# Another order for the early work of a gated-linear-attention and GLU kernel, with some casts and products on other engines

## Chip, cores and metric

One core of one Trainium2 chip. The metric is the device time of a run in microseconds (us); of several runs the median is taken.

## The reference

An attention with a decaying state, and a gated linear unit behind it. B, H, S, D are 4, 8, 768, 48; the 3072 tokens have 384 channels, and the hidden width is 1536.

```python
for t in range(S):
    state = alpha[:, :, t, :, None] * state + np.einsum('bhd,bhe->bhde', k[:, :, t], v[:, :, t])
    y[:, :, t] = np.einsum('bhd,bhde->bhe', q[:, :, t], state)
x = y.transpose(0, 2, 1, 3).reshape(B * S, H * D)
gate = 1 / (1 + np.exp(-(x @ w_gate)))
out = (gate * (x @ w_val)) @ w_out
```

Everything is float32, and the weights reach the kernel as float64 words.

## The kernel before

**Units.** The attention runs in 24 units: six groups g of 512 tokens by four pairs p of heads. A unit u = 4 g + p loads decay, K and Q (L464, on SyncE's queue), and V (L468, or L472 for the first four). `decays` makes the decay products: a scan from the right (G, L406), a maximum and a reciprocal at chunk borders (L408, L409), a scan from the left (F, L410), the chunk decay (`dec`, L412), and K times G (L414). Q times F follows (L480). On TensorE come the transposition of K (L427), the scores (L492), and the state additions (L497). VectorE masks the scores (L505) and carries the state from chunk to chunk (L520), GpSimd multiplies the states by `dec` (L558 in the first four units, L531 in the next four, L658 later), and TensorE makes the outputs (L571 and L576, or L542 and L546). The first eight units ("early") use chunks of 128 tokens, the rest (`late`) chunks of 64.

**Steps.** The gated unit runs in 72 steps, 12 for a group of tokens. A step multiplies 128 of the 1536 hidden columns: 18 matmuls for gate and value (L693, by way of L236), the sigmoid (L698, ScalarE), the product (L700, VectorE), its split into two float32r halves (L701 ScalarE, L702 VectorE), and nine matmuls back to 384 channels (L710). Every product is made of three matmuls of such halves.

**Weights.** Twelve weight tiles are made in the first 120 us, tile 0 in three pieces of 384 columns and the others in two of 576 (`weight_piece`). A piece is a load (L360), a cast of the upper bits (L363 on VectorE if the piece stands in `CASTS`, else L365 on ScalarE), a shift-and-or (L368, VectorE), a cast (L371, ScalarE) and a subtraction (L378, VectorE).

**Order.** Every piece of work is added to a `Plan` with its engine, its cost in us, a due time or none, and what it reads and writes. `Plan.order` then replays the engines with these costs: each engine takes the ready part with the earliest latest start, and the order of the replay is the order in which each engine's queue is written. Parts with `port` set take turns in the replay: one that would begin while another has the port waits for it. `SHIFTS` adds so many us to the latest start of single parts, which are numbered in the order in which they were added. `QUERIES` and `KEYS` name the early units whose L480 and L414 run on VectorE; elsewhere they run on GpSimd. 29 matmuls on constants (L681) stand in the plan: eight at its start, the others wherever TensorE has nothing ready. Nothing is reordered on the chip: every engine goes through its queue in order.

The lines of the change: costs at L363, L365, L408, L409, L412, L416, L514, L531, L558, L578, L611 and L649; the tuples at L804 to L807.

Of the kernel before, what the change touches and what calls it, by code (L numbers as in the profile page):

```python
# [37 lines left out]
CH, EH = T // C, T // E  # L38
# [163 lines left out]
def pool_(n):  # L202
    return 0.08 + n / 445
# [36 lines left out]
def chunked(ctx, tc, rows, vc, vh, vg, weights_in, out, const, ident, flags, weights, within):  # L240
    nc = tc.nc
    sb = ctx.enter_context(tc.tile_pool(name="sb", bufs=1))
    ps = ctx.enter_context(tc.tile_pool(name="ps", bufs=1, space=bass.MemoryType.PSUM))
    plan = Plan()
# [46 lines left out]
    for tag in ("w11", "w8"):  # L291
        nm, t = borrow(tag, WF + 2)
# [53 lines left out]
    def weight_piece(f, key):  # L346
        cuts = (0, DM, 2 * DM, WF) if f == 0 else (0, WF // 2, WF)
        over = before(f"w{f}") if f >= 6 else []
        for i, (lo, hi) in enumerate(zip(cuts, cuts[1:])):
            n = hi - lo  # L350
            rn, raw = (r_raw if f < 7 else r_raw3).next() if f < NF - 1 else raws[i]
            raw = raw[:, 0:2 * n + 2]
            lower = raw[:, 1:1 + 2 * n].rearrange("p (m j) -> p m j", j=2)[:, :, 0]
            most = raw[:, 2:2 * n + 2].bitcast(BF16).rearrange("p (m h) -> p m h", h=4)[:, :, 0]
            tn, top = (r_top if f < 8 else r_top1).next()
            top = top[:, 0:n]
            high = top.bitcast(F16).rearrange("p (m h) -> p m h", h=2)[:, :, 1]
            ru, rl, rt = (rn, "u"), (rn, "l"), (tn, "a")
            kk = key
            plan.add("sync", (0.475, P * n * 8 / RATE), None, lambda raw=raw, lo=lo, n=n: nc.sync.dma_start(  # L360
                out=raw.bitcast(U16), in_=ahead(weights_in, f, lo, n)), writes=[ru, rl])
            if (f, i) in CASTS:
                plan.add("vector", 0.01 + n / 960, kk, lambda high=high, most=most: nc.vector.tensor_copy(out=high, in_=most), [ru], [rt], port=True)  # L363
            else:
                plan.add("scalar", 0.08 + n / 500, kk, lambda high=high, most=most: nc.scalar.copy(out=high, in_=most), [ru], [rt])  # L365
            high, low = (weights_part(f, part, lo, hi) for part in range(2))
            word = raw[:, 0:n]
            plan.add("vector", 0.07 + n / 960, kk, lambda lower=lower, top=top, word=word: nc.vector.scalar_tensor_tensor(  # L368
                out=word, in0=lower, scalar=13, in1=top, op0=ALU.logical_shift_right, op1=ALU.bitwise_or), [rt, ru], [rl], port=True)
# [29 lines left out]
    def decays(u, size, t, inn, tin):  # L399

        n, nch = T, T // size
        a0, az, kT = tin[:, 0:nch], tin[:, A_Z:A_K], tin[:, A_K:A_Q]
        over = ["later"] if size == E else []
        (gn, G), (fn, F), (g0n, G0), (decn, dec) = r_G.next(), r_F.next(), r_G0.next(), r_dec.next()
        G0, dec = G0[:, 0:nch], dec[:, 0:nch]
        plan.add("vector", scan(n), t["G"], lambda: nc.vector.tensor_tensor_scan(  # L406
            out=G[:, ::-1], data0=az[:, n:0:-1], data1=d1g[size], initial=0.0, op0=ALU.mult, op1=ALU.add), [(inn, "a"), *over], [gn], port=True)
        plan.add("vector", 0.1, t["G"], lambda: nc.vector.tensor_tensor(out=G0, in0=G[:, 0:n:size], in1=tiny[:, 0:nch], op=ALU.max), [gn], [g0n], port=True)  # L408
        plan.add("vector", 0.1, t["G"], lambda: nc.vector.reciprocal(out=d1f[:, 0:n:size], in_=G0), [g0n], ["d1f"])  # L409
        plan.add("vector", scan(n), after(t["G"], 0.01), lambda: nc.vector.tensor_tensor_scan(  # L410
            out=F, data0=az[:, 0:n], data1=d1f, initial=0.0, op0=ALU.mult, op1=ALU.add), ["d1f", (inn, "a")], [fn], port=True)
        plan.add("vector", 0.1, t["dec"], lambda: nc.vector.tensor_tensor(out=dec, in0=a0, in1=G[:, 0:n:size], op=ALU.mult), [gn, (inn, "a")], [decn], port=True)  # L412
        e = "vector" if u in KEYS else "gpsimd"
        plan.add(e, vec(n) if u in KEYS else pool_(n), t["kt"], lambda: getattr(nc, e).tensor_tensor(  # L414
            out=kT, in0=kT, in1=G, op=ALU.mult), [gn, (inn, "r")], [(inn, "k")], port=True)
        plan.add("scalar", 0.2, t["flag"], lambda: nc.scalar.copy(out=starts[:, u, 0:nch], in_=G[:, 0:n:size]), [gn], [("start", u)])  # L416
        return fn, F, decn, dec

    def bound(u, t, fn, F):
# [39 lines left out]
    def unit(u, g, p, t):  # L459

        n, nch = T, CH
        inn, tin = r_in.next()
        for lo, hi, marks in ((0, A_K, "a"), (A_K, WIDTH, "rkq")) if u < NP else ((0, WIDTH, "arkq"),):
            plan.add("sync", (0.475, P * (hi - lo) * 4 / RATE), t["load"], lambda lo=lo, hi=hi: nc.sync.dma_start(  # L464
                out=tin[:, lo:hi], in_=rows[g, p, :, lo:hi]), writes=[(inn, m) for m in marks])
        if g:
            vn, v = r_v.next()
            plan.add("sync", (0.475, P * CH * 2 * D * 4 / RATE), after(t["load"], 0.2), lambda: nc.sync.dma_start(  # L468
                out=v.rearrange("p c j e -> p (c j e)"), in_=vc[g, p]), writes=[(vn, "v")])
        else:  # L470
# [60 lines left out]
        plan.add("gpsimd", pool_(nch * D), t["sd"], lambda: nc.gpsimd.tensor_tensor(  # L531
            out=sd, in0=st[:, 0:nch], in1=dec.rearrange("p (c o) -> p c o", o=1).broadcast_to([P, nch, D]), op=ALU.mult), [sn, decn], [(sdn, x) for x in range(4)])

        yield
# [17 lines left out]
    def in_place(p, t, qT, inn, vw, A, sd, st, dec):  # L552
# [2 lines left out]
        sd = sd.rearrange("p j c e -> p (j c e)")[:, 0:CH * 2 * D].rearrange("p (c e) -> p c e", e=2 * D)  # L555
        for j in range(2):
            r = slice(R * j, R * j + R)
            plan.add("gpsimd", pool_(CH * D), t["sd"], lambda j=j, r=r: nc.gpsimd.tensor_tensor(  # L558
                out=sd[r, :, D * j:D * j + D], in0=st[r, 0:CH], in1=dec[r].rearrange("p (c o) -> p c o", o=1).broadcast_to([R, CH, D]), op=ALU.mult),
                [sn, decn], [(sdn, 2 * j), (sdn, 2 * j + 1)])  # L560
        blocks = [divmod(3 * p + i, 4) for i in range(3)]
# [16 lines left out]
        plan.add("tensor", (0.9, 0.5), t["out"], from_states, [(inn, "q"), *((sdn, x) for x in range(4))], banks)  # L578
# [10 lines left out]
    def late(u, g, p, t):  # L589
# [18 lines left out]
            plan.add("sync", (0.475, R * EH * D * 4 / RATE), after(t["more"], 0.2), lambda j=j: nc.sync.dma_start(  # L608
                out=vs[other[j], j].rearrange("p c e -> p (c e)"), in_=vh[g, p, j]), writes=[(vsn, j)])
        for j in range(2):  # L610
            plan.add("vector", 0.71, t["q"], lambda j=j: nc.vector.tensor_tensor(  # L611
                out=A[own[j], j], in0=A[own[j], j], in1=F[own[j]], op=ALU.mult), [fn], [(an, 2 + j)], port=True)
        bound(u, t, fn, F)

# [31 lines left out]

        st, sn = sts[p], ("st", p)
        done = EH if u >= EARLY + NP else CH
        plan.add("gpsimd", 0.28, t["S"], lambda: nc.gpsimd.tensor_copy(out=st[:, 0, :], in_=st[:, done, :]), writes=[sn])  # L649

        def states():
            for c in range(EH):
# [148 lines left out]


SUMS = ()
CASTS = ((0, 2), (3, 1), (5, 0), (5, 1), (7, 0), (7, 1), (10, 1))  # L804
QUERIES = (0, 4, 5, 6)
KEYS = (0,)
SHIFTS = ((0, -5), (37, -1), (40, -2), (45, -1), (49, -1), (62, 1), (96, 2), (118, 1), (124, -1), (126, 2), (127, 2), (134, -1), (142, -2), (152, 4), (153, -6), (164, 13), (192, -2), (222, -5), (227, 1), (235, -1), (261, -4), (280, 2), (289, -5), (303, 4), (304, 3), (307, 7), (314, 17), (323, 3), (328, 4), (331, 13), (340, -6), (350, 4), (378, 12), (389, 2), (414, 8), (421, 7), (422, 9), (435, 5), (436, -1), (443, 9), (448, 4), (500, 3), (543, 1), (552, 4), (643, -1), (784, -4), (817, 4), (849, 2), (885, 2))  # L807
WARM = 29
APART = 24

# [143 lines left out]
```

## Time and profile before

| | |
|---|---|
| median of 3 runs | 552.58 us (552.45 to 552.87) |
| the profiled execution | 552.85 us, of which the span is 551.0 us |
| TensorE busy | 538.3 us, 98% of the span |
| VectorE busy | 328.7 us, 60% |
| ScalarE busy | 179.2 us, 33% |
| GpSimd busy | 93.8 us, 17% |
| HBM traffic | 41.16 MB read, 4.72 MB written |
| mean granted clock of TensorE | 0.993 |

The profile is one execution. PE is TensorE's matmuls, PEld its weight loads, DVE is VectorE, ACT ScalarE, POOL GpSimd, SP SyncE (it issues the loads). Times count from the start of the span. PEclk is the granted clock of TensorE as a share of its full one. A row of the timeline gives start, duration, engine, line, operation, out<-in by tile names, and how many instructions it merges; in square brackets stands the engine's idle time before it and whose end it waited for. A tile can bear the name of the memory that it borrows (`first_w`, `first_x`).

### The profile page before, as it was taken

The page shows a single profiled execution, that of the slowest core. Times are in us where ns is not written, and L with a number is a line of the kernel's source. Part 1 is how long each engine was busy: PE and PEld are TensorE (multiplying, and loading weights), DVE is VectorE, ACT ScalarE, POOL GpSimd, SP SyncE. Part 2 cuts the span into 40 slices and gives each one's busy share as a digit, 9 for nine tenths or more (in the row PEclk, how much of TensorE's full clock was granted, in tenths as well). Part 3 has the DMA queues.
Part 4 walks back from the last instruction along what each step waited for, and adds up shares of the span by engine and source line. Part 5 has one row for each costly group of instructions (what it writes and reads, how often), then busy time and mean ns, then how long its engine had stood idle before and what let it go on. Part 6 is the DMA issues. An engine that isn't in the chain of part 4 may idle for free.

```text
span 551.0 us, 10327 instructions
## 1 busy us (share of the span) xinstructions
PE 538.3 (98%) x4215; PEld 435.3 (79%) x4215; DVE 328.7 (60%) x629; ACT 179.2 (33%) x337; POOL 93.8 (17%) x113
## 2 busy tenths in 40 slices
PE   8998999999999999999999999999999999999994
PEld 4776877888888888888888888888888888888883
DVE  7789998977657567648547557566566342222221
ACT  2445645552223232323223323223323222211221
POOL 5650132002202202112012022022021010000000
PEclk9998999999999999999999999999999999999998
DMA  8645875721402311403203303213211000100001
GB/s 312 259 130 171 262 253 150 229 89 61 151 20 83 101 43 59 159 1 102 90 13 101 136 23 103 66 36 101 104 56 49 2 16 16 57 0 1 0 2 62
DMA packets 21576, 50.57 MB, mean 92 GB/s; under 512 B 3344, under 2 KB 8464, under 8 KB 21520
## 3 DMA queue, kind: packets, MB, share of 16 engines
q1 hardware_dynamic: 21520, 49.83, 28.0%
q8 instruction: 35, 0.57, 0.4%
q14 instruction: 21, 0.17, 0.1%
HBM read 41.16 MB, written 4.72 MB: 83 GB/s over the span
## 4 chain that ended last, share of the span: by engine, by line
PE 96%; DVE 1%; POOL 1%; issue 0%; ACT 0%; POOLq 0%; ACTq 0%
PE gv L236 54%; PE po L710 28%; PE gv L670 3%; PE gv L427 2%; PE at L624 2%; PE gv L681 1%; PE at L630 1%; PE po L576 1%; PE at L492 1%; PE gv L542 1%; PE gv L546 1%; PE po L571 1%; PE gv L497 0%; POOL first_w L480 0%; PE po L681 0%
## 5 line engine op out<-in xcount | busy, mean ns | idle before, releaser
L236 PE MATMUL gv<-x,w 128*128 128x512 f32 x1296 | 316.1, 390 | 0.0
L236 PEld LDWEIGHTS gv<-x,w 128*128 128x128 f32 x1296 | 242.5, 188 | 52.2 <-issue 0.8
L700 DVE TENSOR_TENSOR gv<-gv,sg 128x512 f32<-128x512 f32 x72 | 50.3, 699 | 156.7 <-PE gv L236 153.0
L710 PE MATMUL po<-hh,w 128*128 128x512 f32 x432 | 115.8, 399 | 1.0 <-ACT w L371 0.9
L710 PEld LDWEIGHTS po<-hh,w 128*128 128x128 f32 x432 | 80.1, 189 | 18.8 <-ACT w L371 1.0
L701 ACT CAST hh<-gv 128x512 fp32r<-128x512 f32 x72 | 42.2, 586 | 152.5 <-DVE gv L700 145.5
L658 POOL TENSOR_TENSOR vs<-st,dec 64x384 f32<-64x384 f32 x32 | 36.4, 1139 | 277.1 <-DVE st L653 261.5
L698 ACT ACTIVATE sg<-gv 128x512 f32<-128x512 f32 x72 | 43.0, 597 | 120.2 <-PE gv L236 119.6
L702 DVE TENSOR_TENSOR hl<-gv,hh 128x512 fp32r<-128x512 f32 x72 | 49.6, 689 | 24.5 <-ACT hh L701 22.4
L710 PE MATMUL po<-hl,w 128*128 128x512 f32 x216 | 63.7, 393 | 0.0
L710 PEld LDWEIGHTS po<-hl,w 128*128 128x128 f32 x216 | 40.7, 189 | 8.6
L653 DVE SCALAR_TENSOR_TENSOR st<-st,dec,at 128x48 f32<-128x48 f32 x128 | 33.9, 265 | 4.2
L414 POOL TENSOR_TENSOR in<-in,G 128x512 f32<-128x512 f32 x21 | 28.7, 1367 | 39.3 <-DVE G L406 33.0
L406 DVE TENSOR_TENSOR_SCAN G<-in,d1g 128x512 f32<-128x512 f32 x22 | 34.1, 1551 | 2.1 <-DMA in<-in_rows_dram 2.1
L640 DVE TENSOR_TENSOR A<-at,mask 64x256 f32<-64x256 f32 x64 | 26.9, 420 | 7.8 <-PE at L630 7.4
L410 DVE TENSOR_TENSOR_SCAN F<-in,d1f 128x512 f32<-128x512 f32 x22 | 27.8, 1264 | 0.6
L611 DVE TENSOR_TENSOR A<-A,F 64x512 f32<-64x512 f32 x32 | 23.4, 731 | 0.5
L420 ACT ACTIVATE F<-F 128x512 f32<-128x512 f32 x23 | 14.5, 631 | 16.9 <-DVE A L611 15.3
L670 PE MATMUL gv<-A,vs 128*48 128x64 f32 (+1 forms) x512 | 17.6, 221 | 0.0
L670 PEld LDWEIGHTS gv<-A,vs 128*48 128x48 f32 (+1 forms) x512 | 15.2, 123 | 2.8 <-DVE A L640 2.2
L431 ACT COPY kn<-gv 128x512 f32<-128x512 f32 x21 | 12.3, 586 | 12.2 <-PE gv L427 10.0
L438 ACT COPY yt<-gv 128x512 f32<-128x512 f32 x20 | 11.7, 586 | 11.7 <-PE gv L670 7.4
(130 smaller groups left out, 338.7 us busy)
## 6 DMA issues: line engine op xcount, KB each, us to landing
in<-in_rows_dram SPq DMA_DIRECT2D x16, 516.5 KB, 3.8
raw<-in_w_dram SPq DMA_DIRECT2D x14, 577.0 KB, 4.6
first_w<-in_w_dram SPq DMA_DIRECT2D x8, 577.0 KB, 4.5
out_dram<-raw SPq DMA_DIRECT2D x18, 256.0 KB, 2.3
A<-in_rows_dram SPq DMA_DIRECT2D x32, 128.0 KB, 3.3
v<-in_vc_dram SPq DMA_DIRECT2D x20, 192.0 KB, 4.3
in<-in_rows_dram SPq DMA_DIRECT2D x4, 772.5 KB, 5.8
vs<-in_vh_dram SPq DMA_DIRECT2D x32, 96.0 KB, 2.8
```

The lines of the kernel that those rows point to most:

```text
L236: nc.tensor.matmul(out=dst, lhsT=lhs(a, i), rhs=rhs(b, i), start=(n == 0 and i == 0), stop=(n == len(todo) - 1 and i == NK - 1))
L406: plan.add("vector", scan(n), t["G"], lambda: nc.vector.tensor_tensor_scan(out=G[:, ::-1], data0=az[:, n:0:-1], data1=d1g[size], initial=0 ...
L410: plan.add("vector", scan(n), after(t["G"], 0.01), lambda: nc.vector.tensor_tensor_scan(out=F, data0=az[:, 0:n], data1=d1f, initial=0.0, o ...
L414: plan.add(e, vec(n) if u in KEYS else pool_(n), t["kt"], lambda: getattr(nc, e).tensor_tensor(out=kT, in0=kT, in1=G, op=ALU.mult), [gn, ( ...
L653: nc.vector.scalar_tensor_tensor(out=st[:, c + 1, :], in0=st[:, c, :], scalar=dec[:, c:c + 1], in1=pas[c % 2][1][:, T // 2 + c // 2 * D:T ...
L658: plan.add("gpsimd", pool_(EH * D), t["sd"], lambda j=j: nc.gpsimd.tensor_tensor(out=vs[own[j], j], in0=st[own[j], 0:EH], in1=dec[own[j]]. ...
L670: nc.tensor.matmul(out=py[R * j:R * j + D, cs], lhsT=vs[r, j, c, :], rhs=A[r, j, cs], start=True, stop=True)
L698: plan.add("scalar", act(T), first(0.3), lambda: nc.scalar.activation(out=sg, in_=got["g"][1][:, 0:T], func=AF.Sigmoid), [got["g"][0]], [sgn])
L700: plan.add("vector", vec(T), first(0.4), lambda: nc.vector.tensor_tensor(out=pv, in0=pv, in1=sg, op=ALU.mult), [sgn], [pvn])
L701: plan.add("scalar", act(T), first(0.45), lambda: nc.scalar.copy(out=hh, in_=pv), [pvn], [hhn])
L702: plan.add("vector", vec(T), first(0.5), lambda: nc.vector.tensor_tensor(out=hl, in0=pv, in1=hh, op=ALU.subtract), [pvn, hhn], [hln])
L710: nc.tensor.matmul(out=pso_now[m][1][:, 0:T], lhsT=weights.part("o", b, f)[:, m * P:(m + 1) * P], rhs=h[a][:, 0:T], start=(f == 0 and i == ...
```

## The change

It alters costs by which the plan orders, the `port` mark of VectorE's weight casts, the engine of some casts and products, and all of `SHIFTS` but two entries. No operation, tile or transfer is added or taken away. The diff, with the shifts cut after the first entries (before there are 49, after 58):

```diff
             if (f, i) in CASTS:
-                plan.add("vector", 0.01 + n / 960, kk, lambda ...: nc.vector.tensor_copy(out=high, in_=most), [ru], [rt], port=True)
+                plan.add("vector", 0.04 + n / 1700, kk, lambda ...: nc.vector.tensor_copy(out=high, in_=most), [ru], [rt])
             else:
-                plan.add("scalar", 0.08 + n / 500, kk, lambda ...: nc.scalar.copy(out=high, in_=most), [ru], [rt])
+                plan.add("scalar", n / 800, kk, lambda ...: nc.scalar.copy(out=high, in_=most), [ru], [rt])
...
-        plan.add("vector", 0.1, t["G"], ... op=ALU.max ...)
-        plan.add("vector", 0.1, t["G"], ... reciprocal ...)
+        plan.add("vector", 0.08, t["G"], ... op=ALU.max ...)
+        plan.add("vector", 0.09, t["G"], ... reciprocal ...)
...
-        plan.add("vector", 0.1, t["dec"], ...)
+        plan.add("vector", 0.07, t["dec"], ...)
...
-        plan.add("scalar", 0.2, t["flag"], ... starts ...)
+        plan.add("scalar", 0.14, t["flag"], ... starts ...)
...
-            plan.add("gpsimd", 0.28, t["G"], ... st[:, nch, :] ...)
+            plan.add("gpsimd", 0.18, t["G"], ... st[:, nch, :] ...)
...
-        plan.add("gpsimd", pool_(nch * D), t["sd"], ...)
+        plan.add("gpsimd", 0.57, t["sd"], ...)
...
-            plan.add("gpsimd", pool_(CH * D), t["sd"], ...)
+            plan.add("gpsimd", 0.57, t["sd"], ...)
...
-        plan.add("tensor", (0.9, 0.5), t["out"], from_states, ...)
+        plan.add("tensor", (1.0, 0.5), t["out"], from_states, ...)
...
-            plan.add("vector", 0.71, t["q"], ... in1=F[own[j]] ...)
+            plan.add("vector", 0.61, t["q"], ... in1=F[own[j]] ...)
...
-        plan.add("gpsimd", 0.28, t["S"], ... st[:, done, :] ...)
+        plan.add("gpsimd", 0.18, t["S"], ... st[:, done, :] ...)
...
-CASTS = ((0, 2), (3, 1), (5, 0), (5, 1), (7, 0), (7, 1), (10, 1))
-QUERIES = (0, 4, 5, 6)
-KEYS = (0,)
-SHIFTS = ((0, -5), (37, -1), (40, -2), (45, -1), (49, -1), (62, 1), (96, 2), (118, 1), (124, -1), (126, 2), ...
+CASTS = ((0, 0), (0, 1), (3, 0), (4, 0), (5, 1), (6, 0), (6, 1), (7, 0), (8, 0))
+QUERIES = (0, 1, 2, 6)
+KEYS = (0, 2, 4, 6)
+SHIFTS = ((13, -1), (43, 3), (63, -2), (64, 1), (65, -4), (69, 1), (84, -1), (97, -2), (98, -2), (99, -1), (107, -1), (125, 13), (128, 2), ...
```

In numbers of parts, 0 to 152 belong to the fill matmuls' first entries and units 0 to 3, 153 to 277 to the weight pieces, and those from 278 on to the later units and the steps. Of the 58 shifts 13, 14 and 31 lie in these three.

## Rows read from the trace of the kernel before

**Rows 1.** The page: TensorE's busy time, and the chain that ended last, by engine.

```profile
PE 538.3 (98%) x4215; PEld 435.3 (79%) x4215; DVE 328.7 (60%) x629; ACT 179.2 (33%) x337; POOL 93.8 (17%) x113
...
PE 96%; DVE 1%; POOL 1%; issue 0%; ACT 0%; POOLq 0%; ACTq 0%
```

**Rows 2.** Windows: length, PE, PEld, DVE, ACT, POOL busy, PEclk, DMA share, GB/s.

```profile
20.00:25.00 5.00, 4.08 (x69) 3.39 (x64) 4.24 (x10) 1.41 (x4) 4.04 (x4) 1.00 0.59 209
...
45.00:50.00 5.00, 3.40 (x36) 2.49 (x37) 5.00 (x12) 2.99 (x7) 0.00 (x0) 0.85 0.47 126
50.00:55.00 5.00, 5.00 (x21) 3.80 (x21) 4.92 (x11) 2.78 (x4) 1.00 (x2) 0.81 0.69 227
...
7.00:20.00 13.00, 13.00 (x183) 9.12 (x183) 9.72 (x22) 4.69 (x11) 7.03 (x8) 1.00 1.03 397
5.00:55.00 50.00, 46.01 (x505) 33.88 (x505) 44.08 (x92) 21.99 (x45) 20.16 (x26) 0.97 0.63 220
...
57.00:130.00 73.00, 72.99 (x511) 58.41 (x512) 62.58 (x110) 38.43 (x69) 11.98 (x11) 1.00 0.59 191
130.00:544.00 414.00, 413.90 (x3165) 340.23 (x3163) 217.95 (x419) 115.13 (x219) 57.51 (x57) 1.00 0.18 57
```

**Rows 3.** Timeline, unit 1: its Q product, fill matmuls, scores and first mask.

```profile
14.08 2.17 POOL L480 TENSOR_TENSOR in<-in,F 128x512 f32<-128x512 f32 x1 [2.35 <-DVE dec L412]
...
16.10 1.04 PE L681 MATMUL gv<-ident 128*128 128x512 bf16 x4
...
17.06 0.37 PE L492 MATMUL gv<-in 48*128 48x128 f32 x1
...
18.26 0.69 DVE L505 TENSOR_TENSOR A<-gv,mask 128x512 f32<-128x512 f32 x1 [1.94 <-PE at L492]
```

**Rows 4.** Timeline, unit 2: its Q product, scores and masks.

```profile
20.88 2.10 POOL L480 TENSOR_TENSOR first_w<-first_w,first_x 128x512 f32<-128x512 f32 x1 [2.36 <-DVE dec L412]
...
23.04 1.16 PE L492 MATMUL gv<-first_w 48*128 48x128 f32 x16 [0.85 <-POOL first_w L480]
...
24.23 1.29 DVE L505 TENSOR_TENSOR first_x<-gv,mask 128x512 f32<-128x512 f32 x2 [0.65 <-PE gv L492]
```

**Rows 5.** Timeline: a K product of unit 4 and `dec` beside it; `dec` alone (unit 0).

```profile
33.31 1.69 POOL L414 TENSOR_TENSOR in<-in,G 128x512 f32<-128x512 f32 x1 [1.95 <-DVE G L406]
33.80 1.23 DVE L412 TENSOR_TENSOR dec<-in,G 128x4 f32<-128x4 f32 x1
...
4.96 0.16 DVE L412 TENSOR_TENSOR dec<-in,G 128x4 f32<-128x4 f32 x1
```

**Rows 6.** One line's instructions (ns min/median/max): L414 on either engine, L480 on VectorE.

```profile
L414 POOL TENSOR_TENSOR in<-in,G x21: 1267/1290/1693, 8.7 to 403.9; 128x512 f32<-128x512 f32 x21
L414 DVE TENSOR_TENSOR in<-in,G x1: 661/661/661, 5.2 to 5.2; 128x512 f32<-128x512 f32 x1
...
L480 DVE TENSOR_TENSOR in<-in,F x4: 667/686/687, 8.4 to 70.6; 128x512 f32<-128x512 f32 x4
```

**Rows 7.** Casts on either engine, GpSimd's state products (one line each); then a timeline.

```profile
L363 DVE CAST first_w<-first_w x2: 382/441/500, 46.2 to 55.9; 128x384 f16<-128x384 bf16 x1, 128x576 f16<-128x576 bf16 x1
...
L365 ACT CAST top<-raw x7: 633/854/877, 14.1 to 117.2; 128x576 f16<-128x576 bf16 x6, 128x384 f16<-128x384 bf16 x1
...
L531 POOL TENSOR_TENSOR vs<-st,dec x4: 506/591/882, 39.4 to 92.8; 128x192 f32<-128x192 f32 x4
...
50.39 0.50 DVE L363 CAST first_w<-raw 128x576 f16<-128x576 bf16 x1
50.62 0.59 POOL L531 TENSOR_TENSOR vs<-st,dec 128x192 f32<-128x192 f32 x1 [10.40 <-DVE st L520]
```

**Rows 8.** Timeline: unit 4's scores, the first back products, and six such at the end.

```profile
45.07 1.16 PE L492 MATMUL at<-in 48*128 48x128 f32 x16 [0.77 <-DVE in L480]
...
48.21 3.20 PE L710 MATMUL po<-hh,w 128*128 128x512 f32 x6 [0.86 <-ACT w L371]
...
537.62 1.52 PE L710 MATMUL po<-hh,w 128*128 128x512 f32 x6
```

More of the change, by code (lines that the diff above doesn't have):

```diff
@@ L362, in weight_piece @@
             if (f, i) in CASTS:
-                plan.add("vector", 0.01 + n / 960, kk, lambda high=high, most=most: nc.vector.tensor_copy(out=high, in_=most), [ru], [rt], port=True)
+                plan.add("vector", 0.04 + n / 1700, kk, lambda high=high, most=most: nc.vector.tensor_copy(out=high, in_=most), [ru], [rt])
             else:
-                plan.add("scalar", 0.08 + n / 500, kk, lambda high=high, most=most: nc.scalar.copy(out=high, in_=most), [ru], [rt])
+                plan.add("scalar", n / 800, kk, lambda high=high, most=most: nc.scalar.copy(out=high, in_=most), [ru], [rt])
             high, low = (weights_part(f, part, lo, hi) for part in range(2))
@@ L407, in decays @@
             out=G[:, ::-1], data0=az[:, n:0:-1], data1=d1g[size], initial=0.0, op0=ALU.mult, op1=ALU.add), [(inn, "a"), *over], [gn], port=True)
-        plan.add("vector", 0.1, t["G"], lambda: nc.vector.tensor_tensor(out=G0, in0=G[:, 0:n:size], in1=tiny[:, 0:nch], op=ALU.max), [gn], [g0n], port=True)
-        plan.add("vector", 0.1, t["G"], lambda: nc.vector.reciprocal(out=d1f[:, 0:n:size], in_=G0), [g0n], ["d1f"])
+        plan.add("vector", 0.08, t["G"], lambda: nc.vector.tensor_tensor(out=G0, in0=G[:, 0:n:size], in1=tiny[:, 0:nch], op=ALU.max), [gn], [g0n], port=True)
+        plan.add("vector", 0.09, t["G"], lambda: nc.vector.reciprocal(out=d1f[:, 0:n:size], in_=G0), [g0n], ["d1f"])
         plan.add("vector", scan(n), after(t["G"], 0.01), lambda: nc.vector.tensor_tensor_scan(
             out=F, data0=az[:, 0:n], data1=d1f, initial=0.0, op0=ALU.mult, op1=ALU.add), ["d1f", (inn, "a")], [fn], port=True)
-        plan.add("vector", 0.1, t["dec"], lambda: nc.vector.tensor_tensor(out=dec, in0=a0, in1=G[:, 0:n:size], op=ALU.mult), [gn, (inn, "a")], [decn], port=True)
+        plan.add("vector", 0.07, t["dec"], lambda: nc.vector.tensor_tensor(out=dec, in0=a0, in1=G[:, 0:n:size], op=ALU.mult), [gn, (inn, "a")], [decn], port=True)
         e = "vector" if u in KEYS else "gpsimd"
@@ L415, in decays @@
             out=kT, in0=kT, in1=G, op=ALU.mult), [gn, (inn, "r")], [(inn, "k")], port=True)
-        plan.add("scalar", 0.2, t["flag"], lambda: nc.scalar.copy(out=starts[:, u, 0:nch], in_=G[:, 0:n:size]), [gn], [("start", u)])
+        plan.add("scalar", 0.14, t["flag"], lambda: nc.scalar.copy(out=starts[:, u, 0:nch], in_=G[:, 0:n:size]), [gn], [("start", u)])
         return fn, F, decn, dec
@@ L513, in unit @@
         if g:
-            plan.add("gpsimd", 0.28, t["G"], lambda: nc.gpsimd.tensor_copy(out=st[:, 0, :], in_=st[:, nch, :]), writes=[sn])
+            plan.add("gpsimd", 0.18, t["G"], lambda: nc.gpsimd.tensor_copy(out=st[:, 0, :], in_=st[:, nch, :]), writes=[sn])
         else:
@@ L530, in unit @@
         sd = sd[:, 0, 0:CH, :]
-        plan.add("gpsimd", pool_(nch * D), t["sd"], lambda: nc.gpsimd.tensor_tensor(
+        plan.add("gpsimd", 0.57, t["sd"], lambda: nc.gpsimd.tensor_tensor(
             out=sd, in0=st[:, 0:nch], in1=dec.rearrange("p (c o) -> p c o", o=1).broadcast_to([P, nch, D]), op=ALU.mult), [sn, decn], [(sdn, x) for x in range(4)])
@@ L557, in in_place @@
             r = slice(R * j, R * j + R)
-            plan.add("gpsimd", pool_(CH * D), t["sd"], lambda j=j, r=r: nc.gpsimd.tensor_tensor(
+            plan.add("gpsimd", 0.57, t["sd"], lambda j=j, r=r: nc.gpsimd.tensor_tensor(
                 out=sd[r, :, D * j:D * j + D], in0=st[r, 0:CH], in1=dec[r].rearrange("p (c o) -> p c o", o=1).broadcast_to([R, CH, D]), op=ALU.mult),
@@ L576, in from_scores @@
                     nc.tensor.matmul(out=at(i, c), lhsT=vw[:, c, lo:lo + 32], rhs=A[:, j, c * C:(c + 1) * C], start=False, stop=(c == CH - 1 and (i, j) != (1, 0)))
-        plan.add("tensor", (0.9, 0.5), t["out"], from_states, [(inn, "q"), *((sdn, x) for x in range(4))], banks)
+        plan.add("tensor", (1.0, 0.5), t["out"], from_states, [(inn, "q"), *((sdn, x) for x in range(4))], banks)
         for j in range(2):
@@ L610, in late @@
         for j in range(2):
-            plan.add("vector", 0.71, t["q"], lambda j=j: nc.vector.tensor_tensor(
+            plan.add("vector", 0.61, t["q"], lambda j=j: nc.vector.tensor_tensor(
                 out=A[own[j], j], in0=A[own[j], j], in1=F[own[j]], op=ALU.mult), [fn], [(an, 2 + j)], port=True)
@@ L648, in late @@
         done = EH if u >= EARLY + NP else CH
-        plan.add("gpsimd", 0.28, t["S"], lambda: nc.gpsimd.tensor_copy(out=st[:, 0, :], in_=st[:, done, :]), writes=[sn])
+        plan.add("gpsimd", 0.18, t["S"], lambda: nc.gpsimd.tensor_copy(out=st[:, 0, :], in_=st[:, done, :]), writes=[sn])
         def states():
@@ L803 @@
 SUMS = ()
-CASTS = ((0, 2), (3, 1), (5, 0), (5, 1), (7, 0), (7, 1), (10, 1))
-QUERIES = (0, 4, 5, 6)
-KEYS = (0,)
-SHIFTS = ((0, -5), (37, -1), (40, -2), (45, -1), (49, -1), (62, 1), (96, 2), (118, 1), (124, -1), (126, 2), (127, 2), (134, -1), (142, -2), (152, 4), (153, -6), (164, 13), (192, -2), (222, -5), (227, 1), (235, -1), (261, -4), (280, 2), (289, -5), (303, 4), (304, 3), (307, 7), (314, 17), (323, 3), (328, 4), (331, 13), (340, -6), (350, 4), (378, 12), (389, 2), (414, 8), (421, 7), (422, 9), (435, 5), (436, -1), (443, 9), (448, 4), (500, 3), (543, 1), (552, 4), (643, -1), (784, -4), (817, 4), (849, 2), (885, 2))
+CASTS = ((0, 0), (0, 1), (3, 0), (4, 0), (5, 1), (6, 0), (6, 1), (7, 0), (8, 0))
+QUERIES = (0, 1, 2, 6)
+KEYS = (0, 2, 4, 6)
+SHIFTS = ((13, -1), (43, 3), (63, -2), (64, 1), (65, -4), (69, 1), (84, -1), (97, -2), (98, -2), (99, -1), (107, -1), (125, 13), (128, 2), (157, -5), (162, 1), (165, -2), (180, 5), (184, 1), (187, 2), (190, 7), (197, 5), (200, 2), (207, -2), (210, 2), (222, 2), (230, 7), (253, 2), (278, 5), (279, 3), (283, 5), (299, 2), (317, 1), (330, -4), (335, 3), (336, 1), (338, 5), (342, -1), (344, -1), (359, -2), (366, -4), (367, 7), (390, 1), (401, -3), (418, -4), (433, -2), (434, 6), (435, -1), (491, -2), (494, 7), (532, 2), (552, 4), (566, 7), (581, -8), (582, 5), (659, 1), (706, 2), (817, 4), (898, 14))
 WARM = 29
```

## The prediction

> **What bounds the kernel now.** I read the page first, for the engine that ends last. TensorE is busy for 538.3 of 551.0 us, and 96% of the chain that ended last lies on it [rows 1]. Such a share is a mean, so the windows come next, to see where TensorE stands still or runs slowly. From 130 to 544 us it is busy for 413.90 of 414.00 us at clock 1.00, and from 57 to 130 us for 72.99 of 73.00 [rows 2]. There nothing is to be had: whatever VectorE or GpSimd does there is hidden while TensorE always has work. The change can pay only before 57 us, and there it pays in one way: when the last stop of TensorE ends sooner, everything behind it moves up by as much.
>
> From 5 to 55 us TensorE is busy for 46.01 of 50 us, so it stands still for 3.99 us. Its clock is 0.85 in 45 to 50 us and 0.81 in 50 to 55 us [rows 2], a mix of the two levels, 1.2 and 2.4 GHz, behind the longest stop of the stage. Measured against full speed that is (0.15 + 0.19) x 5 = 1.70 us. It shows in single rows too: six back products at 48.21 us last 3.20 us, six at the end 1.52 [rows 8], 1.68 us more.
>
> Which engine holds TensorE up there? VectorE: it is busy for 44.08 of the 50 us, and for 9.92 of the last 10; ScalarE for 21.99 of 50, GpSimd for 20.16 [rows 2]. So VectorE's queue sets when the first weights and units are done, and I count what the change takes from it and puts on it up to 57 us. The timeline shows where it still stands idle. In unit 1 GpSimd makes the Q product, from 14.08 to 16.25 us, which is 2.17 us; the scores follow at 17.06, behind four fill matmuls, and VectorE waits 1.94 us for them [rows 3]. In unit 2 it is the same: 2.10 us, TensorE idle for 0.85, VectorE for 0.65 [rows 4].
>
> The length of these products is the second thing to see. Alone, GpSimd takes 1.27 to 1.29 us for a product of this size [rows 6], so some 0.85 us of each is waiting, while VectorE's scan runs. It also works the other way round: at 33.80 us VectorE's tiny `dec` product takes 1.23 us beside GpSimd's K product, where it takes 0.16 alone [rows 5]. The two engines do take turns, and a product left to GpSimd is not free for VectorE: it can cost it 1.07 us, more than the 0.66 that VectorE needs for it itself.
>
> **The change part by part.** The sum is made on the profiled execution: 552.85 us, that is 551.0 of span and 1.85 around it. It lies 0.27 above the median of 552.58.
>
> Q products. Units 1 and 2 move to VectorE (two of 0.69 us [rows 6], +1.38), units 4 and 5 leave it (both lie before 57 us, -1.38). VectorE's sum stays. What moves is the wait: F of unit 1 is followed at once by a product of 0.69 instead of 2.17 us, and the scores come some 1.5 us sooner. While they run, VectorE has the scan of unit 2 to do, so the 1.94 and 0.65 us of waiting go: -2.59 [rows 3, 4]. What is late next is VectorE's own queue, which is what I count.
>
> Unit 4's Q product goes the other way. TensorE's scores waited 0.77 us for it on VectorE [rows 8]; on GpSimd it takes 1.29 - 0.69 = 0.60 us longer if GpSimd has its turn at once, 2.17 - 0.69 = 1.48 if it meets a scan as in unit 1, and nothing if the order puts step work of TensorE ahead. The two ends are 0 and +1.48; I take +0.30, half of the undisturbed price, because GpSimd has little else there (no work at all in 45 to 50 us, 1.00 of 5 behind it [rows 2]) but the wait shows that TensorE's cover is thin. Behind the waiting product on GpSimd stand only the state products of the same unit. Unit 5's comes at a place where the queue of TensorE is full; nothing.
>
> K products. Units 2 and 4 move to VectorE before 57 us: 2 x 0.66 = +1.32 [rows 6]. Unit 4's no longer takes VectorE's turn: 1.23 - 0.16 = -1.07 [rows 5]. Unit 2's ran on GpSimd beside state updates, where no such delay is seen: 0. Unit 6's lies behind 57 us, where TensorE has cover.
>
> Casts. Up to 57 us VectorE has one of 384 columns and two of 576; afterwards two of 384 and two of 576 ((3, 0) and (4, 0) for (3, 1) and (5, 0)). The difference is one of 0.38 us [rows 7]: +0.38. ScalarE loses the same casts at 0.63 and 0.85 us each [rows 7], but it is idle for more than half of the stage [rows 2], so I put that at nothing. Behind 57 us VectorE has four before and five after, under TensorE's cover.
>
> Does a VectorE cast need the turn? The plan no longer says so. The row to look at is the cast at 50.39 us, 0.50 long, with a GpSimd state product at 50.62: that takes 0.59 us instead of 0.51 [rows 7]. It is held up by 0.08 at the most, not by the 0.27 for which the cast still runs. I take 0.08 for one meeting, and one or two meetings: 0.1, inside the rounding. The Trainium skill (SBUF — State Buffer, Who interferes with whom) speaks against the change here: it counts casts among the operations that take the shared ports for the whole instruction when they run in a two-port mode. By it the state product would have started 0.27 us late, and the trace shows 0.08, so it holds at most in part; the sum would be worse by up to one GpSimd product for a cast that meets one, which is weighed as a rival.
>
> Loads. SyncE's queue gets another order in units 1, 3 and 4 and the first weights. The DMA engines are full from 7 to 20 us (share 1.03 [rows 2]), so a load that moves up pushes others back by its own length. No row shows what that does; the ends are -0.65 and +1.94, the least and the most of what one late input has cost VectorE in these units [rows 3, 4]. I take 0 and keep the ends for the range. New prices of small operations, and shifts behind 57 us, change order only; TensorE's cover hides them, and if it were gone a wait there would cost what it lasts.
>
> The sum: -2.59 + 0.30 + 1.32 - 1.07 + 0.38 = -1.66, so about 551.2 for the profiled execution and **550.9** as a median. The clock loss of 1.70 us is kept in it, since the stop at 45 to 50 us is not shown to go.
>
> **The rivals.** About 0.2%, 1.1 us, is what a measurement of this kernel can tell from no change.
>
> First, **VectorE becomes free early enough that the stop at 45 to 50 us goes**. TensorE idles 1.60 us there [rows 2]. A stop of 0.92 us from 20 to 25 us left the clock at 1.00 [rows 2]. If the later one becomes as short, the 1.70 us come back as well: 550.9 - 1.7 = 549.2. For it: the stop is no longer than the gain. Against it: in that window VectorE is busy for all of the 5.00 us, so the gain has to come through every unit ahead. Chance 0.15.
>
> Second, **the gain is used up on the way**. The wait for scores of unit 1 is replaced by others: VectorE finishes masks sooner and then waits for weight pieces or for unit 3, whose Q product stays on GpSimd. Also here: the casts take turns after all. From 20 to 25 us GpSimd is busy for 4.04 of 5 us [rows 2]; two casts of tile 0 that each stand behind a product of 1.29 us would cost up to 2.58. The Trainium skill's rule above (SBUF — State Buffer, Who interferes with whom) would have it so. Either way of the two eats some 1.4 of the 1.66 us: 552.3. For it: the chain of 5 to 55 us crosses four engines, and a freed one finds the next late. Against it: both waits named are GpSimd's, and go. Chance 0.20, a quarter of that for the casts.
>
> Third, on the other side, **a second stop of TensorE, with its clock**. TensorE arrives sooner at 45 to 60 us, where VectorE is full (9.92 of 10 us) and now holds more work ahead of it; a weight part or unit 4's Q product on GpSimd is not ready, and TensorE stops once more for as long as at 45 to 50 us and falls to the lower clock again. Price 1.60 + 1.70 = 3.30, less the gain of 1.66: 552.58 + 1.64 = 554.2. It decides when new waits before 60 us exceed the gain, and doubly when one stop is as long as that at 45 us. For it: two products of that stage go to the slower engine, and the order is found by prices, not by this trace. Against it: the new prices lie nearer to rows than the old (ScalarE's cast of 576 columns at 0.72 against 1.23; the row says 0.85 [rows 7]). Chance 0.18.
>
> **How the numbers follow.** The forecast has 0.47, with 549.9 to 551.4 as its own range. Faster by over 0.2% is the forecast and the first rival, 0.62; within 0.2% the second, 0.20; slower the third, 0.18. The range of 8 in 10 runs from 548.9, a little under the first rival, to 553.4, through nearly all of the second; the third and the tail below are left out.
>
> **What would show it.** Right: unit 1's Q product on VectorE with 0.69 us, its scores near 15 to 16 us instead of 17.06; no wait of VectorE for scores over 0.7 us before 30 us; no `dec` of 1.2 us in unit 4; TensorE without a stop from some 55 us on. Wrong: a VectorE cast stretched beyond 0.60 us beside GpSimd; an idle time of TensorE before 60 us above 4 us in all, or the clock under 0.81 in some window behind 45 us; unit 4's scores waiting on GpSimd for more than 1.5 us; any idle time of TensorE behind 60 us that is more than a few tenths.

## The result and the profile after

The changed kernel takes 546.31 us (median of four runs, 545.69 to 547.11) against 552.52 for the kernel before on the same chip: a ratio of 0.9889, 95% interval 0.9872 to 0.9906. It is faster by 6.2 us, where 1.7 were forecast; 546.31 lies below the range. The profiled execution took 546.50 us, its span 544.7.

First the windows of the changed kernel, with the columns of [rows 2]: length, PE, PEld, DVE, ACT, POOL busy, PEclk, DMA share, GB/s.

```profile
7.00:20.00 13.00, 12.06 (x180) 8.74 (x181) 12.80 (x27) 3.40 (x9) 5.45 (x6) 1.00 1.04 404
20.00:25.00 5.00, 5.00 (x87) 4.16 (x82) 4.96 (x15) 2.40 (x6) 2.66 (x3) 1.00 0.67 236
...
30.00:35.00 5.00, 4.28 (x63) 3.54 (x63) 5.00 (x11) 2.37 (x5) 0.82 (x3) 1.00 0.22 42
...
45.00:50.00 5.00, 4.77 (x47) 3.96 (x46) 5.00 (x12) 3.17 (x7) 0.75 (x1) 1.00 0.34 115
50.00:55.00 5.00, 5.00 (x46) 3.93 (x45) 4.50 (x9) 3.19 (x5) 0.50 (x2) 1.00 0.79 241
...
5.00:55.00 50.00, 48.12 (x549) 36.71 (x548) 47.45 (x100) 23.53 (x48) 17.69 (x23) 1.00 0.67 236
...
57.00:130.00 73.00, 73.00 (x515) 59.09 (x514) 65.10 (x115) 36.46 (x69) 12.74 (x13) 1.00 0.55 179
130.00:538.00 408.00, 408.00 (x3138) 335.14 (x3136) 212.89 (x413) 113.33 (x215) 55.14 (x54) 1.00 0.19 57
```

As [rows 2] did, these say that TensorE has no gap behind 57 us. Between 45 and 55 us the gain is seen at once: TensorE idles 0.23 us instead of 1.60, and the clock stays at 1.00 where it had been 0.85 and 0.81. Between 5 and 55 us the idle time falls from 3.99 to 1.88 us, and 1.70 us of clock come back. Fill matmuls stand where TensorE has nothing else to do, so their time counts with the idle time. The windows of L681 alone (length, PE and PEld busy, PEclk, DMA share, GB/s), before and after:

```profile
5.00:55.00 50.00, 6.44 (x22) 1.97 (x20) 0.97 0.63 220
...
5.00:55.00 50.00, 5.85 (x22) 1.95 (x20) 1.00 0.67 236
```

Idle and filled time together fall from 10.43 to 7.73 us. These 2.70 us and the clock make 4.40 of the 6.3 us by which the span is shorter. Another 0.4 us lies behind the last matmul, which ends at 543.90 of 551.0 us before and at 538.00 of 544.7 after. Where the other 1.5 us are is not shown.

Where the stop of 44 to 49 us came from shows in rows that the prediction did not look at. This is the timeline of the kernel before: the last piece of weight tile 0 (384 columns), with its cast, shift, and subtraction; a cast of tile 2 on ScalarE; two loads on SyncE, the first for tile 5, the second for tile 2; and TensorE's state additions of unit 5.

```profile
46.20 0.38 DVE L363 CAST first_w<-first_w 128x384 f16<-128x384 bf16 x1
46.31 2.90 SPq L360 DMA_DIRECT2D first_w<-in_w_dram  x2
...
46.78 0.56 PE L497 MATMUL gv<-v,kn 128*48 128x48 f32 x16 [0.55 <-ACT kn L431]
...
47.07 0.55 DVE L368 SCALAR_TENSOR_TENSOR first_w<-first_w,first_w 128x384 uint32<-128x384 uint32 x1
...
48.07 0.85 ACT L365 CAST first_w<-raw 128x576 f16<-128x576 bf16 x1
...
48.31 0.55 DVE L378 TENSOR_TENSOR w<-first_w,w 128x384 fp32r<-128x384 f32 x1
```

This piece holds two buffers. Its shift (L368) reads the buffer for upper bits that the first piece of tile 2 needs for its cast: that cast follows at 48.07. Its subtraction (L378) ends the use of the raw tile that the second piece of tile 2 is loaded to: the second of the two loads goes out at about 49, behind 48.86. So the back products of step 0 and all of step 2 stand behind one piece, which `SHIFTS` had put off by 13 us ((164, 13), the cast). TensorE's stop is in fact three: 0.77 us for unit 4's Q product [rows 8], 0.55 for a copy of K (L431), and 0.86 for this piece (L371 [rows 8]). Only the third names the piece; at the other two TensorE's queue has no step work that could go ahead. The same pieces in the changed kernel, with the first back products:

```profile
33.65 0.55 DVE L368 SCALAR_TENSOR_TENSOR first_w<-first_w,first_w 128x384 uint32<-128x384 uint32 x1
...
36.72 0.55 DVE L378 TENSOR_TENSOR w<-first_w,w 128x384 fp32r<-128x384 f32 x1
...
37.29 0.34 SPq L360 DMA_DIRECT2D first_w<-in_w_dram  x1
...
37.50 0.85 ACT L365 CAST first_w<-raw 128x576 f16<-128x576 bf16 x1
...
40.29 0.62 PE L710 MATMUL po<-hh,w 128*128 128x512 f32 x2
```

The shift runs 13.4 us sooner, the cast of tile 2 10.6, and back products stand at 40.29 us, where the first of them had been at 48.21 [rows 8].

The units look much as forecast. The timeline of the changed kernel, units 1 and 2 (Q product, scores):

```profile
15.11 0.65 DVE L480 TENSOR_TENSOR in<-in,F 128x512 f32<-128x512 f32 x1
...
16.43 0.37 PE L492 MATMUL gv<-in 48*128 48x128 f32 x1
...
20.28 0.68 DVE L480 TENSOR_TENSOR first_w<-first_w,first_x 128x512 f32<-128x512 f32 x1
...
21.23 1.16 PE L492 MATMUL gv<-first_w 48*128 48x128 f32 x16
```

The scores come 0.63 and 1.81 us sooner than in [rows 3, 4], and VectorE waits for neither. Unit 1's stand at 16.43 us, not at 15 to 16, since TensorE first ends the outputs of unit 0. A cast does what the prediction held to be unlikely. The timeline of the changed kernel again, GpSimd's K product of unit 3 and the first two casts of tile 0:

```profile
20.43 1.65 POOL L414 TENSOR_TENSOR first_w<-first_w,G 128x512 f32<-128x512 f32 x1 [2.14 <-issue]
...
21.06 1.27 DVE L363 CAST top<-raw 128x384 f16<-128x384 bf16 x1
...
22.40 0.38 DVE L363 CAST first_w<-raw 128x384 f16<-128x384 bf16 x1
```

The first cast takes 1.27 us where 0.38 is its time alone, as the second shows, and GpSimd's product ends at 22.08, just ahead of the cast's end at 22.33. So VectorE's cast waited for its turn. It is no single case: at 80.91 us a cast of 576 columns takes 1.20 us behind a GpSimd product of 1.28, where 0.50 is its time alone [rows 7].

### The profile page after: what moved, and what is told of

The parts are those of the page before. It is cut to its first block, busy times and chain, and to the rows that moved or that the text cites. A ratio compares the mean times of both kernels' runs of the same rounds, so it can differ in the third digit from the quotient of the medians.

```text
span 544.7 us, 10318 instructions
## 1 busy us (share of the span) xinstructions
PE 534.5 (98%) x4215; PEld 433.8 (80%) x4215; DVE 329.6 (61%) x634; ACT 176.1 (32%) x335; POOL 90.2 (17%) x110
## 4 chain that ended last, share of the span: by engine, by line
PE 90%; DVE 5%; DMA 2%; ACT 0%; issue 0%; SPq 0%; ACTq 0%; DVEq 0%
PE gv L236 53%; PE po L710 27%; PE gv L670 3%; PE gv L427 2%; PE at L624 2%; DMA raw<-in_w_dram 1%; PE at L630 1%; DMA in<-in_rows_dram 1%; PE at L492 1%; PE gv L542 1%; PE gv L546 1%; DVE F L410 1%; DVE st L520 1%; DVE G L406 0%; DVE w L378 0%; DVE A L505 0%
## 5 line engine op out<-in xcount | busy, mean ns | idle before, releaser
L698 ACT ACTIVATE sg<-gv 128x512 f32<-128x512 f32 x72 | 43.0, 597 | 119.8 <-PE gv L236 119.7
L710 PE MATMUL po<-hl,w 128*128 128x512 f32 x216 | 62.4, 390 | 0.0
L406 DVE TENSOR_TENSOR_SCAN G<-in,d1g 128x512 f32<-128x512 f32 x22 | 33.0, 1505 | 3.7 <-DMA in<-in_rows_dram 3.7
L414 POOL TENSOR_TENSOR in<-in,G 128x512 f32<-128x512 f32 x19 | 26.0, 1368 | 27.6 <-DVE G L406 17.5
L611 DVE TENSOR_TENSOR A<-A,F 64x512 f32<-64x512 f32 x32 | 25.2, 788 | 0.8 <-DMA A<-in_rows_dram 0.2
L420 ACT ACTIVATE F<-F 128x512 f32<-128x512 f32 x23 | 14.6, 635 | 17.9 <-DVE A L611 13.4
L431 ACT COPY kn<-gv 128x512 f32<-128x512 f32 x21 | 12.3, 586 | 11.6 <-PE gv L427 10.4
L438 ACT COPY yt<-gv 128x512 f32<-128x512 f32 x20 | 11.7, 586 | 11.2 <-PE gv L670 8.6
```

The costliest lines, as they stand in the source:

```text
L698: plan.add("scalar", act(T), first(0.3), lambda: nc.scalar.activation(out=sg, in_=got["g"][1][:, 0:T], func=AF.Sigmoid), [got["g"][0]], [sgn])
L710: nc.tensor.matmul(out=pso_now[m][1][:, 0:T], lhsT=weights.part("o", b, f)[:, m * P:(m + 1) * P], rhs=h[a][:, 0:T], start=(f == 0 and i == ...
```

## The experiments

The first question was whether engines or order make the gain. A kernel of this kind can tell them apart: the order in which the parts are issued can be written down as a list (`ORDER`) and kept, while engines change, or the other way round.

```diff
-        for n in self.order():
+        for n in ORDER:
             self.parts[n][3]()
```

**Engines alone.** `ORDER` is that of the kernel before; `CASTS`, `QUERIES` and `KEYS` are those of the changed one.

> The order of all queues is that of the kernel before, only the 19 casts and products stand on the engines of the changed one. If the engines carry the gain (the prediction's sum), the time falls by the 1.7 us forecast or more, to 551 or below, and VectorE's waits for the scores of units 1 and 2 (1.94 and 0.65 us) go. If the order of the weight pieces carries it, the time stays within 1.1 us of 552.5: TensorE's stops at 36.9, 44.3, 46.2 and 47.3 us remain, since the last piece of weight tile 0 is still made at 46 us.

Measured: 553.61 us, ratio 1.0030 (1.0017 to 1.0043). Slower, by 1.3 us. What TensorE waited for in this run (us in total, times, longest):

```profile
PE at L492 <- POOL in L480: 1.7, 1, 1.7
...
PE po L710 <- ACT w L371: 1.1, 1, 1.1
```

and its windows:

```profile
45.00:50.00 5.00, 2.70 (x34) 1.97 (x35) 3.89 (x9) 3.65 (x8) 1.28 (x2) 0.78 0.39 121
50.00:55.00 5.00, 5.00 (x13) 3.89 (x14) 4.63 (x10) 2.85 (x4) 0.52 (x2) 0.54 0.65 184
```

VectorE's waits for the scores of units 1 and 2 went, as the engines' side of the question had it (0.5 us for unit 0 is left), and it bought nothing: the weight pieces had kept their places. Unit 4's Q product on GpSimd holds TensorE for 1.7 us instead of 0.77 [rows 8]; TensorE idles 2.30 us from 45 to 50 us, and the clock is 0.78 there and 0.54 behind it.

**Order alone.** `ORDER` is that of the changed kernel; the three tuples are those of before.

> The order of the changed kernel, with all casts and products on the engines of before. If the engines carry the gain, 551 us or more. If the order of the weight pieces carries it, 547 to 549 us: TensorE has back products of step 0 from some 41 us on, and the window from 45 to 50 us keeps clock 1.00; at most the 1.5 us by which Q products of units 1 and 2 come later are lost.

Measured: 546.78 us, ratio 0.9907 (0.9888 to 0.9925), an interval that overlaps the changed kernel's. So by the ratios 5.1 of 6.2 us come with the order. What the engines of 19 casts and products add to it is some 1 us or nothing: a later set of runs of the changed kernel, below, gave 0.9905.

**The clock alone.** The kernel before with nine fill matmuls in the stops of 44 to 48 us, three behind unit 5's transposition, two behind unit 4's scores, four behind unit 5's state additions.

```diff
+    def fill(k):
+        bn, bank = r_po.tiles[k % NM]
+        plan.add("tensor", (0.2135, 1.0), None, lambda: nc.tensor.matmul(
+            out=bank, lhsT=wz, rhs=..., start=True, stop=True))
```

> The kernel before with nine fill matmuls on constants in TensorE's three stops between 44 and 48.2 us (three, two and four), nothing else. If the loss of 1.7 us behind the stop is the clock's, which falls because TensorE stands still, the clock stays at 1.00 there and the time falls by 1.0 to 1.7 us, to 551. If the six slow back products at 48.2 us wait for weights (only the record makes them look slow), the time stays within 0.5 us of 552.5.

Measured: 551.12 us, ratio 0.9977 (0.9966 to 0.9987), 1.2 us. In its windows the clock is at 1.00 throughout:

```profile
45.00:50.00 5.00, 4.79 (x44) 2.99 (x45) 5.00 (x11) 2.84 (x6) 0.00 (x0) 1.00 0.53 130
50.00:55.00 5.00, 4.73 (x33) 3.33 (x33) 4.92 (x11) 2.55 (x4) 1.00 (x2) 1.00 0.65 231
```

No piece is sooner, and yet most of the 1.70 us come back. Five of the six back products of [rows 8] now take 1.43 us:

```profile
48.76 1.43 PE L710 MATMUL po<-hh,w 128*128 128x512 f32 x5 [0.19 <-DVE w L378]
```

So they were slow by the clock, which fell behind the stops. The plain runs of the kernel before say the same. Beside these experiments it ran 75 times between 549.8 and 553.6 us. In 18 of these runs the mean granted clock was 0.996 or more, and their median is 550.6 us; in 47 it was 0.993 or less, and theirs is 552.6. So it seems that the same stops are not always followed by the loss (no trace of such a run is kept), and that it costs some 2 us where they are. The run with the engines alone had 0.993 or less in all of its ten runs; against the 47 it costs 1.0 us.

**The weight pieces moved by hand.** In the order of before, the last piece of tile 0 is made beside tile 1, tile 2 ahead of tile 3, and step 0's back products and step 2's gate products move up with them. Two casts, of (0, 2) and (3, 1), also go from VectorE to ScalarE.

> The order of before, with three edits: the last piece of weight tile 0 is made beside tile 1 (some 33 us instead of 46), tile 2 is made ahead of tile 3, and TensorE's back products of step 0 and its gate products of step 2 are moved up to where these pieces allow. If the weight pieces carry the gain, the stops from 44 to 48 us and the low clock go: 2 to 4 us faster, 548.5 to 550.5. If the units carry it (scores, Q products), no gain beyond 1.1 us, since VectorE has the same work and only other pieces are late.

Measured: 553.30 us, ratio 1.0027 (1.0013 to 1.0040). Not faster, but its windows say where it failed:

```profile
45.00:50.00 5.00, 5.00 (x47) 3.88 (x46) 3.17 (x8) 1.38 (x3) 0.00 (x0) 1.00 0.40 121
50.00:55.00 5.00, 2.82 (x35) 1.84 (x33) 4.66 (x9) 3.17 (x6) 1.14 (x2) 1.00 0.41 121
55.00:60.00 5.00, 4.34 (x12) 3.43 (x13) 4.31 (x7) 3.59 (x7) 0.00 (x0) 0.66 0.93 325
```

The stop of 45 to 50 us is gone, and a new one of 2.18 us stands at 50 to 55, with the clock behind it at 0.66. TensorE waited there 1.7 us for a sigmoid (L698) that stood on ScalarE behind casts whose inputs were late, and 1.2 us for the second piece of tile 2. A second form, with the pieces of tiles 0 to 5 in the order of their steps and that sigmoid moved up, came out worse. In it the casts of (0, 2), (3, 1), and tile 5 go to ScalarE, and those of tile 4 to VectorE:

> The second form of the edit that left the time unchanged: the order of before, but all pieces of weight tiles 0 to 5 in the order of their steps (tile 2 whole ahead of tile 3, tile 4 ahead of 5), the sigmoid of step 2 right behind its gate product on ScalarE, and TensorE's value product of step 2 ahead of step 3. If TensorE's stops of 44 to 56 us are pieces and steps out of order, they go with the low clock: 549 us or less. If VectorE's work for units 4 and 5 is what is late, a stop of over 2 us stays somewhere before 60 us and the time stays at 551.5 or above.

Measured: 554.51 us, ratio 1.0060 (1.0042 to 1.0078). TensorE's longest waits:

```profile
PE gv L236 <- ACT yt L438: 1.7, 1, 1.7
...
PE gv L236 <- ACT w L371: 1.4, 1, 1.4
```

The copy L438, which frees a bank of PSUM (the memory that TensorE writes to), now stood on ScalarE behind a cast that waited 1.9 us for its load. Pieces moved in two or three queues turned into waits in the others, above all on ScalarE, which had more casts to make as well; what part of the loss these casts are, no run separates.

**The one shift out.** So the edit was made where the plan could follow: in the kernel before one entry of `SHIFTS` goes, and the cast it belongs to goes to ScalarE. Everything is ordered anew.

```diff
-CASTS = ((0, 2), (3, 1), (5, 0), ...
-SHIFTS = (..., (153, -6), (164, 13), (192, -2), ...
+CASTS = ((3, 1), (5, 0), ...
+SHIFTS = (..., (153, -6), (192, -2), ...
```

> The kernel before with one entry of SHIFTS taken out (the 13 us by which the cast of the last piece of weight tile 0 was put off) and that cast on ScalarE; the plan orders everything anew. That piece holds a buffer which the first piece of tile 2 needs for its cast, and one which the second piece needs for its load. If this one late piece is behind the stops of 44 to 52 us, tile 2 follows it by some 5 us sooner and 548 to 550 us come out. If the order must be found as a whole, 551 us or more.

Measured: 548.29 us, ratio 0.9927 (0.9910 to 0.9943): 4.1 us from one entry, with all that the plan does in answer. The cast's engine alone is not it, since the run with the engines alone had that cast on ScalarE too and gained nothing. The timeline of this run: that piece's shift and subtraction, the load behind it, and the back products of step 0; then a window.

```profile
35.62 0.55 DVE L368 SCALAR_TENSOR_TENSOR first_w<-first_w,first_w 128x384 uint32<-128x384 uint32 x1
...
40.44 0.86 DVE L378 TENSOR_TENSOR w<-first_w,w 128x384 fp32r<-128x384 f32 x1
...
41.37 0.33 SPq L360 DMA_DIRECT2D first_w<-in_w_dram  x1
...
43.54 1.52 PE L710 MATMUL po<-hh,w 128*128 128x512 f32 x6
...
35.00:40.00 5.00, 3.43 (x30) 2.44 (x29) 4.00 (x10) 3.82 (x8) 1.42 (x2) 1.00 0.40 118
```

Six back products take 1.52 us, as at full clock in [rows 8], and TensorE is busy for all of 40 to 60 us. It still idles 1.57 us from 35 to 40 us, and there the clock stays at 1.00. Not all of the 4.1 us is the idle time: the four runs had a mean clock of 0.996 to 0.998, and at such a clock the kernel before takes 550.6 us, 2.3 us more. By this measure the other 1.8 us are the clock's.

**Where in time.** These kernels issue the first parts in one order and all others in the other, on the engines of before.

> Engines of before. The first 176 parts (some 32 us, units 0 to 3) stand in the order of before, all others in that of the changed kernel. If the gain lies in the order of weight pieces and steps behind 32 us, 546.5 to 548.5 us. If it lies in the order of units 0 to 3, 551 us or more.

> Engines of before; the first 198 parts (38 us of the plan) in the order of before, the rest in that of the changed kernel. If the gain lies behind 38 us (tile 0's last piece, tile 2), 546.5 to 548.5 us; if between 32 and 38 us, 550.5 or more.

> As the run before, with 221 parts (42 us) in the order of before. The last piece of tile 0 is then made right behind 42 us: with the late piece as the cause about half of the gain is left, 548.5 to 550.5 us; if the gain lies behind 42 us, 548 or below; if ahead of it, 551.5 or above.

> As the run before, with 242 parts (47 us) in the order of before. If the late piece is the cause, the stops and the low clock of 44 to 52 us are there again and no more than 1 us of the gain is left: 551 to 553 us. If what comes behind 47 us carries the gain, 549 or below.

> Engines of before. The first 179 parts (some 31 us) stand in the order of the changed kernel, all others in that of before. If the gain lies behind 32 us, 550.5 to 553 us, with a stop of TensorE from 44 to 50 us as before. If it lies in units 0 to 3, 549 us or less.

| first part | then | median us | ratio (interval) |
|---|---|---|---|
| old to 32 us | new | 547.70 | 0.9930 (0.9903 to 0.9958) |
| old to 38 us | new | 549.25 | 0.9935 (0.9918 to 0.9952) |
| old to 42 us | new | 550.21 | 0.9958 (0.9940 to 0.9976) |
| old to 47 us | new | 551.95 | 0.9986 (0.9971 to 1.0001) |
| new to 31 us | old | 553.62 | 1.0021 (1.0002 to 1.0040) |

On these engines the new order throughout gave 0.9907. The longer the old order stands, the less is left: most of what is won is won between 32 and 47 us, and nothing by the new order of units 0 to 3 if the old one follows. The second row lies between the two ranges that were expected, so not all of that is behind 38 us. The profiled run of the 42 us kernel, with 553.04 us the slowest of its five, shows a stop of its own (TensorE busy 3.06 of 5 us from 50 to 55 us), so that row mixes the late piece with the seam between two orders.

**What was still open** after these: the other 2 us, and the cast that waited. The first 31 us in the new order, ahead of the order with one shift out:

> The first 31 us in the order of the changed kernel, the rest in the order that the kernel before takes with the one shift out; engines of before. If the rest of the gain lies in units 0 to 3, 546 to 547 us. If it lies in the order behind them, 548 us or more, as without these 31 us.

Measured: 550.21 us, ratio 0.9960 (0.9944 to 0.9975), slower than without these 31 us. Seven of the twelve runs, with a mean clock of 0.994 or 0.995, took 550.05 to 551.23 us; the five with 0.997 or 0.998 took 548.35 to 549.11, about what the run with one shift out takes. None reaches 547. So the other 2 us are not in units 0 to 3 by themselves; which of the later parts carry them stays open.

The two casts of tile 0, on ScalarE in the changed kernel's order, at first alone and then beside the changed kernel on one chip:

```diff
-CASTS = ((0, 0), (0, 1), (3, 0), ...
+CASTS = ((3, 0), ...
```

> The changed kernel, in its order, with the casts of the first two pieces of weight tile 0 on ScalarE as before. In the changed kernel the first of them took 1.27 us on VectorE beside a K product of GpSimd, where 0.38 is its time alone. If casts take turns with GpSimd and VectorE's time there reaches the end, 545 to 546 us. If VectorE's 0.9 us there is covered, the same as the changed kernel within 0.7 us.

> The changed kernel itself, as the mark for the two runs beside it: 545.5 to 547 us.

> The changed kernel with the casts of the first two pieces of weight tile 0 on ScalarE. If the 0.9 us that VectorE waits for its turn there reaches the end, 0.5 to 1.0 us below the changed kernel in the same rounds; if it is covered, within 0.4 us of it.

Measured: at first 545.44 us, ratio 0.9883 (0.9853 to 0.9914); then 545.83 us (545.27 to 546.11), ratio 0.9892 (0.9873 to 0.9911), beside the changed kernel's 546.75 (545.75 to 547.16), ratio 0.9905 (0.9885 to 0.9925). The difference in the same rounds is 0.9 us, as long as the wait of the one cast, 1.27 - 0.38 = 0.89. The intervals against the kernel before overlap, and the first set gives only 0.3 us (0.9883 beside 0.9889). Set beside each other, though, the two sets of six runs share only the stretch of 545.75 to 546.11 us, and their means differ by 0.88 us with a standard error of 0.26. The traces say where it goes: a row and the window of the changed kernel above, and the same window with the two casts on ScalarE:

```profile
30.77 0.73 PE L236 MATMUL gv<-x,w 128*128 128x512 f32 x2 [0.72 <-DVE x L585]
...
30.00:35.00 5.00, 4.28 (x63) 3.54 (x63) 5.00 (x11) 2.37 (x5) 0.82 (x3) 1.00 0.22 42
...
30.00:35.00 5.00, 5.00 (x68) 4.12 (x68) 5.00 (x10) 2.75 (x5) 0.00 (x0) 1.00 0.35 109
```

In both traces of the changed kernel TensorE stands for 0.72 us there behind VectorE (L585), and in both with the casts on ScalarE it does not. So VectorE's time at 21 to 23 us does reach the end; how much of it is the wait and how much the two casts themselves is not separated. This version has the lowest time of all that ran.

## Why the prediction was wrong

**Where it can pay** was right: only before 57 us, and through TensorE's last stop; TensorE has no gap behind it in either kernel.

**The step that failed** is the sum. It counted what changes its engine and put what changes its place at nothing: "New prices of small operations, and shifts behind 57 us, change order only", and of the shifts ahead of 57 us only the loads were looked at. Order alone is worth 5.1 us, engines alone cost 1.3. The prediction took VectorE's 44.08 busy us of 50 to mean that its amount of work sets the end. It does not: the order of that work does. At 46 us VectorE was busy, but with pieces of tile 3 and with units, while the piece on which two buffers, six back products and a whole step hung came last. The rows were there: TensorE's wait at 48.21 names L371 of a weight [rows 8], the change takes the entry (164, 13) out of `SHIFTS`, and the code says that part 164 is that piece's cast. Following that wait back through its buffers would have led to the entry that is worth 4.1 us in the run with one shift out.

**The terms.** The Q products of units 1 and 2: the waits of 1.94 and 0.65 us did go, with the engines alone too, but in that run the time rose, so there the -2.59 was not on the path that sets the end. Unit 4's Q product was put at +0.30, between 0 and 1.48; with the old order it cost 1.7 - 0.77 = 0.9 us and, with more idle time there, more of the clock; in the new order TensorE has other work there and it is hidden. The K products (+1.32 - 1.07) and the added cast (+0.38) are inside the 1 us or nothing that engines are worth in the new order, and no run prices them one by one. The casts of tile 0 are mis-sized: with both on ScalarE the kernel takes 0.9 us less.

**The clock.** That the stop "is not shown to go" kept 1.70 us out of the sum. The first rival had them, at 549.2, and its condition came about; it still lies 2.9 us above what was measured, for it too had the gain come through VectorE's work. The fill run bears out the price (1.2 us with no other change). Its chance of 0.15 was weighed by the length of the stop and by VectorE's busy time, not by what the stop waited for.

**The casts.** From one state product that lost 0.08 us the prediction concluded that casts hardly take turns. The cast at 21.06 us lost 0.89. By the Trainium skill (SBUF — State Buffer, Who interferes with whom) a cast in a two-port mode and a GpSimd instruction shut each other out for the whole instruction, whichever came first; this trace agrees for a cast that comes second, with 1.27 us for 0.38 (no row shows the mode of a cast). In the prediction's row the cast came first, and the state product behind it lost only 0.08 of the 0.27 us that the rule would give.

**The third rival**, a second stop with its clock, did not come about in the changed kernel, but stops like it met the kernels with pieces moved by hand: the first had one of 2.18 us from 50 to 55 us, with the clock at 0.66 behind it.

## What to carry to other kernels

When an engine seems to be the bound because it is always busy, look at what the waiting engine waits for, and follow that one item back through its buffers: a late piece that holds a buffer delays all that is queued for the buffer, and here its due time was worth more than all changes of engine together. A change of order is not a term of zero in a sum; if the kernel is ordered by a plan, make the smallest edit of the plan and let all queues follow, since pieces moved by hand in some queues can become waits in the others. Fill matmuls in a stop that cannot be removed can bring back most of what the clock takes behind it (here 1.2 of 1.7 us); in a trace, count their time as idle time.

## What was not expected of the hardware

A cast on VectorE of 384 columns took 1.27 us beside a GpSimd product, 0.89 more than alone. TensorE's idle time of 0.92 us at 20 to 25 us left the clock at 1.00 [rows 2], and so did 1.57 us at 35 to 40 us in the run with one shift out. In the profiled execution of the kernel before, stops of 0.77, 0.55 and 0.86 us within 4 us were followed by 0.85 and 0.81; with nine fill matmuls in these gaps it stayed at 1.00. In 18 of 75 other runs of the kernel before the mean clock was 0.996 or more, so the same stops seem not always to cost it.
